# Attention into an MLP on one core: the MLP's elementwise work from GpSimd to VectorE, weights two steps ahead, the first block's x prepared over three head pairs

## The chip, the cores and the metric

The kernel runs on one core of a Trainium2 chip. The metric is the time of one execution on the device in microseconds, the median of the runs shown. One execution was also taken with the hardware profiler; every row below is from it. TensorE (PE) multiplies matrices, and its weight loads stand apart as PEld. VectorE is DVE, ScalarE is ACT, GpSimd is POOL, and SyncE (SP) issues nearly all DMA transfers, in the order in which they are written.

## The reference

Attention with a learned bias on relative positions, for 4 batches of 8 heads, 576 positions and 64 columns, and then an MLP over the 2304 tokens:

```python
scores = scale * np.matmul(q, k.transpose(0, 1, 3, 2))
scores = scores + bias.transpose(2, 0, 1)[None, :, :, :]
attn = np.exp(scores - np.max(scores, axis=-1, keepdims=True))
attn = attn / (np.sum(attn, axis=-1, keepdims=True) + 1e-09)
x = np.matmul(attn, v)            # heads side by side: 2304 x 512
h = x @ w_in                      # 512 x 2048
g = np.where(h > 0.0, h, np.exp(np.minimum(h, 0.0)) - 1.0)   # elu
out = g @ w_out                   # 2048 x 512
```

All tensors are float32. The kernel multiplies each in two parts, a high part (the value rounded to the matmul's format) and a low part (the value less its high part), in three products: high by high, high by low, low by high.

## The kernel before

The bias is built first. Attention then runs over 16 head pairs (0 to 15), each in five parts (`order`): scores on TensorE, the sum with the bias and its minimum on VectorE (line 303), the exponential on ScalarE (line 314), a copy of 64 columns on GpSimd (line 319), transposes and the product with v on TensorE. The finished rows go to DRAM (`xd`), as do the sums of the exponentials, inverted (`rd`). Beside that, `aside` decodes one of the 16 weight chunks per head pair and stores it (`wf`).

The MLP works on 3 blocks of 768 tokens (`j`). The 16 chunks of 128 features are taken two at a time, so there are 24 steps (`i`), eight to a block. Steps 0 and 1 (`eight`) compute four products of 12 matmuls. Steps 2 to 23 (`seven`) compute the same with seven products of 6 matmuls (Strassen's scheme), which wants sums of the weights (`make_w`, the tile S) and of x (`sums_x`: T1 to T4). A product goes to one of two PSUM banks (`bank`, h0 and h1); VectorE adds products (the tiles u and c, line 796), the elu is made of a product or sum (`elu_a`: ScalarE's exponential, two VectorE steps), and split into high (`gh`, ScalarE) and low (`gl`, VectorE) by `elu_b`. Between the products of a step stand the 36 matmuls of the second matrix of the step before (`second`, into six banks `acc`); after its last matmul a bank is copied to a tile `os` and stored.

`make_w` runs only in the first block, in step i-1 for step i: two chunks `wa` are loaded (line 490, 0.5 MB each), summed (lines 689 to 694), cast to high parts (ScalarE, line 686), and the low parts are taken (line 687; VectorE takes two, GpSimd three). The result, 2.8 MB, is kept for the step and stored to DRAM (lines 707 and 708); blocks 1 and 2 load it from there (`fetch_w`). The tiles `wa` have two buffers, so that the two chunks of the next step can be loaded only when GpSimd has taken the last low part of this one.

The x of a block is loaded in four pieces (`load_x`: xd into xr, rd into rr), scaled by rr (`scale_x`), split (`high_x`, `low_x`) and summed (`sums_x`). All of it is written out in an order fixed by hand: each engine gets its instructions in the order of the Python code, and waits in that order. `at(i, k, ...)` puts a call after product k of step i.

Of the kernel before, what the change touches and what calls it, by code (L numbers as in the profile page):

```python
# [24 lines left out]
def kernel(  # L25
# [484 lines left out]
    def attention():  # L510
# [16 lines left out]
        late = []  # L527

# [21 lines left out]
        for n in range(NP):  # L550
# [4 lines left out]
            for i, u in enumerate(order):  # L555
# [28 lines left out]
                at = (n - NP + 3, i)  # L584
# [8 lines left out]
                if at == (1, 4):  # L593
                    load_x(0, 1, 0)
                if not last:
                    continue
                if i == 0:
                    load_w(0)
                    load_w(1)
                    scale_x(0, 1, 0, nc.gpsimd)  # L600
                    high_x(0, "B11", xo["B11"], nc.vector.tensor_copy)
                if i == 1:
                    load_x(0, 1, 1)
                    low_x(0, "B11", xo["B11"], nc.gpsimd)
                if i == 2:
                    high_w(0)
                    high_x(0, "B21", xo["B21"], nc.vector.tensor_copy)
                    low_x(0, "B21", xo["B21"], nc.gpsimd)
                if i == 3:
                    low_w(0, nc.vector)  # L610
                    high_x(0, "B12", xo["B12"], nc.vector.tensor_copy)
                    low_x(0, "B12", xo["B12"], nc.gpsimd)
                if i == 4:
                    load_w(2)
                    scale_x(0, 1, 1, nc.gpsimd)
                    high_w(1)
                    decode(dp, plan.get(n), "scale")
        late += pv(NP - 1, 0, (0, 1, 2, 3, 4), xp)
        trans_mid(NP - 1, (2, 3))
        for _ in trans_p(NP - 1, order[-1]):  # L620
            pass
        high_x(0, "B22", xo["B22"], nc.vector.tensor_copy)
# [4 lines left out]

        for op in ("low", "sign", "shift", "add"):
            decode(dp, plan.get(NP - 1), op)
# [7 lines left out]
    def mlp():  # L637
# [7 lines left out]
        slots.extend(halves(xq.tile([P, 2 * XW], F32R, name=f"xs{i}")) for i in range(8 - len(slots)))  # L645
        AN, GN = 2 * 7 * AW, 4 * DM

        third = RW // 2
        wrings = [
            [wq.tile([P, n], F32R, name=f"{x}{i}") for i in range(2)] + [room[:, o:o + n]]  # L650
            for x, n, o in (("wA", AN, third), ("wB", GN, third + AN))
# [18 lines left out]
        def make_w(i):  # L670
# [7 lines left out]
            g = nc.gpsimd  # L678
# [8 lines left out]
            low = lambda k, eng: eng.tensor_sub(parts[k][1], parts[k][2], parts[k][0].bitcast(F32))  # L687
# [8 lines left out]
            low(0, nc.vector)  # L696
            yield
            high(4)
            low(1, nc.vector)
            yield  # L700
            high(2)
            high(3)
            low(4, g)
            yield
            low(2, g)
            low(3, g)
# [6 lines left out]
        def second(i, order):  # L713
            j = i // NQ
            for e, h in order:
# [4 lines left out]
                for t in range(3 * h, 3 * h + 3):  # L720
# [3 lines left out]
                    for x, w in ((gh, wh), (gh, wl), (gl, wh)):  # L724
# [8 lines left out]
                        if count[j, t] == 6 * NQ:  # L733
                            os = ep.tile([P, DM], F32, tag="os", name="os", bufs=2)
# [19 lines left out]

        def bank(k):
            return hp.tile([P, HB], F32, tag=f"h{k % 2}", name=f"h{k % 2}")
# [211 lines left out]
```

## Time and profile before

| | |
|---|---|
| median of 3 runs | 780.82 us (779.89 to 782.12) |
| the profiled execution | 779.03 us, its span 777.2 us |
| TensorE busy | 700.7 us, 90% of the span |
| VectorE busy | 495.7 us, 64% |
| ScalarE busy | 392.6 us, 51% |
| GpSimd busy | 209.9 us, 27% |
| TensorE's granted clock, mean | 0.957 of full |

The span is the time from the first to the last instruction; the execution's own time is 1.8 us longer. In rows of the trace a time in us stands first, then a duration in us, the engine, the line, the operation, what it writes and reads, and how many instructions were put together. In brackets is the engine's idle time just before, and who ended it.

### The profile page before, as it was taken

Reading aid. Unit: us, or ns where it says so; the run is one execution under the profiler, and the core shown is the slowest. Engines: PE = TensorE matmul, PEld = TensorE weight load, DVE = VectorE, ACT = ScalarE, POOL = GpSimd, SP = SyncE. Lnnn points to the kernel's source line nnn. Section 1 sums busy time; section 2 is a strip of 40 time slices with the busy share of each in tenths; the row PEclk is TensorE's granted clock in tenths of the full one; section 3 lists DMA queues with packets and bytes.
Section 4 is the critical chain, followed back from the end, with each engine's and each line's share of the span. In section 5 each row is a group of like instructions: output and inputs, shape, how many; then the busy total and the mean of one; then the engine's idle time right before and its main releaser. Section 6 shows DMA issues by size and latency. Waiting matters only on the chain.

```text
span 777.2 us, 13260 instructions
## 1 busy us (share of the span) xinstructions
PE 700.7 (90%) x4992; PEld 519.1 (67%) x4992; DVE 495.7 (64%) x955; ACT 392.6 (51%) x857; POOL 209.9 (27%) x193
## 2 busy tenths in 40 slices
PE   5998999999999989595888877759999999999996
PEld 3335555556556545495777766648889888989985
DVE  7986777767677764863666665754555676555553
ACT  6997778778877876342333334332222253233222
POOL 0002223222322237613555584530110420000000
PEclk9999999999999998888999987898999999999999
DMA  6997565545554676307666614756765544635302
GB/s 174 221 220 204 180 203 188 182 153 205 182 175 159 232 208 202 126 0 243 235 226 223 226 60 168 285 220 245 257 237 192 219 185 170 252 149 199 152 1 81
DMA packets 49935, 144.58 MB, mean 186 GB/s; under 512 B 13376, under 2 KB 26448, under 8 KB 42192
## 3 DMA queue, kind: packets, MB, share of 16 engines
q1 hardware_dynamic: 49136, 143.44, 55.0%
q8 instruction: 39, 0.64, 0.4%
q10 hardware_dynamic: 736, 0.31, 0.2%
q14 instruction: 24, 0.20, 0.1%
HBM read 92.14 MB, written 40.97 MB: 171 GB/s over the span
## 4 chain that ended last, share of the span: by engine, by line
PE 29%; DMA 10%; POOL 9%; DVE 4%; ACT 3%; issue 2%; SPq 2%; POOLq 0%; ACTq 0%; DVEq 0%
PE acc L726 15%; PE h L763 14%; DMA wa<-wf 8%; DMA out_dram<-os 2%; POOL wA L687 2%; DVE e L744 1%; SPq L490 1%; POOL bias L687 1%; POOL wB L687 1%; POOL S L693 1%; POOL S L694 1%; POOL S L690 1%; DVE e L745 1%; DVE gl L753 1%; POOL S L689 1%
## 5 line engine op out<-in xcount | busy, mean ns | idle before, releaser
L303 DVE CUSTOM_DVE_ANT_0 ss<-ps,bias 128x576 f32<-128x576 f32 x128 | 91.9, 755 | 74.3 <-PE ps L291 60.9
L763 PE MATMUL h<-bias,wA 128*128 128x384 f32 x480 | 104.1, 353 | 30.3 <-DVE c L796 16.8
L744 DVE TENSOR_SCALAR e<-e 128x384 f32<-128x384 f32 x96 | 54.7, 569 | 108.4 <-ACT e L743 108.4
L726 PE MATMUL acc<-wB,gh 128*128 128x512 f32 x360 | 120.6, 404 | 0.0
L763 PEld LDWEIGHTS h<-bias,wA 128*128 128x128 f32 x480 | 88.9, 196 | 43.9 <-issue 18.5
L314 ACT ACTIVATE ss<-ss,nm 128x576 f32<-128x576 f32 x128 | 98.2, 769 | 30.9 <-DVE nm L303 30.8
L291 PE MATMUL ps<-kk,qq 64*128 64x288 f32 (+1 forms) x640 | 108.8, 425 | 2.6 <-DVE nm L303 2.4
L752 ACT CAST gh<-e 128x384 fp32r<-128x384 f32 x96 | 49.3, 513 | 105.2 <-DVE e L745 101.7
L753 DVE TENSOR_TENSOR gl<-e,gh 128x384 fp32r<-128x384 f32 x96 | 68.5, 714 | 46.5 <-ACT gh L752 46.5
L763 PE MATMUL h<-bias 128*128 128x384 f32 x324 | 71.1, 363 | 18.9 <-DVE e L745 11.3
L743 ACT ACTIVATE e<-c 128x384 f32<-128x384 f32 x66 | 34.6, 524 | 102.7 <-DVE c L796 102.7
L763 PEld LDWEIGHTS h<-bias 128*128 128x128 f32 x324 | 62.5, 204 | 26.5 <-DVE e L745 12.6
L291 PEld LDWEIGHTS ps<-kk,qq 64*128 64x128 f32 (+1 forms) x640 | 63.4, 180 | 20.9 <-DVE nm L303 4.7
L726 PEld LDWEIGHTS acc<-wB,gh 128*128 128x128 f32 x360 | 69.5, 195 | 10.4
L319 POOL TENSOR_SCALAR ss<-ss 128x64 f32<-128x64 f32 x64 | 15.9, 249 | 221.0 <-ACT ss L314 221.0
L726 PE MATMUL acc<-wB,gl 128*128 128x512 f32 x180 | 72.4, 402 | 0.0
L726 PE MATMUL acc<-bias,gh 128*128 128x512 f32 x216 | 72.3, 404 | 0.0
L193 PE MATMUL bps<-rel,cs 128*32 128x288 f32 x576 | 44.9, 435 | 11.3 <-ACT rel L183 7.7
L399 PE MATMUL wv<-pta,vv 128*64 128x320 f32 (+1 forms) x320 | 53.6, 448 | 0.0
L355 PEld LDWEIGHTS wt<-ident,ss 64*128 64x128 f32 x1024 | 38.5, 141 | 18.9 <-issue 14.7
L796 DVE TENSOR_TENSOR c<-h,u 128x384 f32<-128x384 f32 x66 | 36.3, 550 | 18.3 <-PE h L763 18.1
L355 PE MATMUL wt<-ident,ss 64*128 64x64 f32 x1024 | 47.5, 231 | 0.0
(104 smaller groups left out, 1109.3 us busy)
## 6 DMA issues: line engine op xcount, KB each, us to landing
wA<-wA SPq DMA_DIRECT2D x15, 1792.0 KB
raw<-in_wd_dram SPq DMA_DIRECT2D x16, 1024.0 KB, 5.1
wB<-wB SPq DMA_DIRECT2D x15, 1024.0 KB, 4.8
wa<-wf SPq DMA_DIRECT2D x20, 512.0 KB, 8.5
bias<-bo SPq DMA_DIRECT2D x16, 576.0 KB, 7.4
bias<-wA SPq DMA_DIRECT2D x5, 1792.0 KB
wf<-da SPq DMA_DIRECT2D x16, 512.0 KB, 2.8
bias<-wB SPq DMA_DIRECT2D x5, 1024.0 KB, 4.6
```

The costliest lines, as they stand in the source:

```text
L193: nc.tensor.matmul(ps[32 * g:32 * g + 32, f, 0:HS], lhsT=W2, rhs=rel[g][:, f * HS:(f + 1) * HS], start=True, stop=True,)
L291: nc.tensor.matmul(banks[e][:, f, 0:HS] if u < NCH else banks[0][r, f, 0:HS], lhsT=qq[r, rows], rhs=kk[r, f * HS:(f + 1) * HS], start=True ...
L303: nc.vector.tensor_tensor_reduce(out=s.rearrange("p (f x) -> p f x", f=2), in0=ps[:, :, 0:HS], in1=bap.rearrange("p (f x) -> p f x", f=2), ...
L314: nc.scalar.activation(s, s, AF.Exp, bias=nm[:, e:e + 1], scale=-1.0, accum_out=sm[:, hp, col:col + 1])
L355: nc.tensor.transpose(banks[r][:, x * TAIL:(x + 1) * TAIL], ss[q, c:c + P], ident[q, q])
L399: nc.tensor.matmul(w[e * D:(e + 1) * D, 0:N], lhsT=l, rhs=r, start=(j == first), stop=(j == end))
L726: nc.tensor.matmul(acc[j, t], lhsT=x[:, t * P:(t + 1) * P], rhs=w, start=(count[j, t] == 1), stop=(count[j, t] == 6 * NQ),)
L744: nc.vector.tensor_scalar(e, e, 1.0, -1.0, op0=ALU.min, op1=ALU.add)
L752: nc.scalar.copy(gh, x)
L753: nc.vector.tensor_sub(gl, x, gh.bitcast(F32))
L763: nc.tensor.matmul(ps, lhsT=a[f][c], rhs=x[y][c], start=(start and k == 0), stop=(stop and k == len(todo) - 1), skip_group_check=not start,)
L796: nc.vector.tensor_add(u[name], x, y)
```

## The change

- `make_w`: the sums and all low parts are VectorE's; it is cut into seven pieces, so that the work is spread over the products of a step, and its stores to DRAM come at the next step's first product.
- `load_w` for step i is called after product 1 of step i-2 (before: product 6, for the first two steps product 3); every other step's chunks have tiles of their own (`wq`), so four chunks can be held.
- `elu_a`: with Relu of -h and the exponential of its negative on ScalarE, and one VectorE instruction (add -1, maximum with h).
- The second block's and third block's `scale_x`, `sums_x` and low parts are VectorE's; two of the seven x operands are split a step ahead (a ninth slot), the others a product earlier.
- The first block's x is loaded and scaled from head pair 12 on, by VectorE, and split on VectorE; its T1 to T4 are made on GpSimd in a row at the MLP's start.
- The last chunk's decoding stands before the last transposes; in step 0 the third and fourth product use PSUM banks of the pool `accp`; `os` has three buffers, not two.

```diff
-    def load_w(fc):
-        wa = wab[fc] = keep.tile([P, WW], F32, tag="wa", name="wa")
+    def load_w(fc, pool=None):
+        wa = wab[fc] = (pool or keep).tile([P, WW], F32, tag="wa", name="wa", bufs=2)
         nc.sync.dma_start(out=wa, in_=wf[fc])
...
+        early = {
+            (-4, 3): [(load_x, 0, 0, 0)],
+            (-3, 0): [(scale_x, 0, 0, 0, nc.vector)],
+            (-3, 1): [(load_x, 0, 0, 1)],
+            (-3, 4): [(scale_x, 0, 0, 1, nc.vector)],
+            (-2, 0): [(load_x, 0, 1, 0), (high_x, 0, "B11", xo["B11"], nc.vector.tensor_copy)],
+            (-2, 2): [(low_x, 0, "B11", xo["B11"], nc.vector)],
+            (-2, 3): [(scale_x, 0, 1, 0, nc.vector)],
+            (-2, 4): [(load_x, 0, 1, 1)],
+            (-1, 0): [(high_x, 0, "B12", xo["B12"], nc.vector.tensor_copy)],
+            (-1, 1): [(low_x, 0, "B12", xo["B12"], nc.vector), (scale_x, 0, 1, 1, nc.vector)],
+            (-1, 2): [(high_x, 0, "B21", xo["B21"], nc.vector.tensor_copy)],
+            (-1, 3): [(low_x, 0, "B21", xo["B21"], nc.vector)],
+        }
...
-                if at == (0, 3):
-                    load_x(0, 0, 0)
-                if at == (1, 0):
-                    scale_x(0, 0, 0, nc.gpsimd)
-                if at == (1, 2):
-                    load_x(0, 0, 1)
-                if at == (1, 3):
-                    scale_x(0, 0, 1, nc.gpsimd)
...
+                for fn, *args in early.get((n - NP, i), ()):
+                    fn(*args)
...
-            g.tensor_add(S1[:, 0], A21, A22)
-            g.tensor_sub(S1[:, 2], A11, A21)
+            v.tensor_add(S1[:, 0], A21, A22)
+            v.tensor_sub(S1[:, 2], A11, A21)
             high(0)
             yield
-            g.tensor_sub(S1[:, 1], S1[:, 0], A11)
-            g.tensor_sub(S1[:, 3], A12, S1[:, 1])
+            v.tensor_sub(S1[:, 1], S1[:, 0], A11)
+            v.tensor_sub(S1[:, 3], A12, S1[:, 1])
+            high(4)
+            yield
+            low(0)
             high(1)
...
-            nc.scalar.activation(e, src, AF.Exp)
-            nc.vector.tensor_scalar(e, e, 1.0, -1.0, op0=ALU.min, op1=ALU.add)
-            nc.vector.tensor_max(e, src, e)
+            nc.scalar.activation(e, src, AF.Relu, scale=-1.0)
+            nc.scalar.activation(e, e, AF.Exp, scale=-1.0)
+            nc.vector.scalar_tensor_tensor(e, e, -1.0, src, op0=ALU.add, op1=ALU.max)
...
-                at(i - 2, 3 if i - 2 < FIRST else 6, load_w, 2 * q + e)
-            for k in range(5):
-                at(i - 1, k if i > FIRST else min(k, 3), next, run)
-            at(i - 1, 5 if i > FIRST else 3, next, run, None)
+                at(i - 2, 1, load_w, 2 * q + e, wq if i % 2 == 0 else keep)
+            for k in range(7):
+                at(i - 1, k if i > FIRST else k // 2, next, run)
+            at(i, 0, next, run, None)
```

What this does to VectorE's order in a step of the first block, here in step 4, from the elu of the third product to the sum c of the sixth. In rows of this kind stand the line, the operation, what it writes and reads, and the size; line 796 of before is line 799 of the changed kernel, 687 is 685 there. Before:

```order
L744 TENSOR_SCALAR e<-e 128x384
L745 TENSOR_TENSOR e<-h_4980,e 128x384
L687 TENSOR_TENSOR wA_4420<-wa,wA_4420 128x512
L753 TENSOR_TENSOR gl<-e,gh 128x384
L796 TENSOR_TENSOR u_5052<-h_5006,p_4989 128x384
L687 TENSOR_TENSOR wB_4422<-wa,wB_4422 128x512
L796 TENSOR_TENSOR c<-h_5061,u_5052 128x384
L744 TENSOR_SCALAR e<-e 128x384
L745 TENSOR_TENSOR e<-c,e 128x384
L753 TENSOR_TENSOR gl<-e,gh 128x384
L796 TENSOR_TENSOR c<-h_5082,u_5052 128x384
```

And with the change, at the same place:

```order
L745 SCALAR_TENSOR_TENSOR e<-e,h_4978 128x384
L691 TENSOR_TENSOR S<-S,wa 128x256
L692 TENSOR_TENSOR S<-wa,S 128x256
L753 TENSOR_TENSOR gl<-e,gh 128x384
L799 TENSOR_TENSOR u_5055<-h_5006,p_4987 128x384
L685 TENSOR_TENSOR wA_4420<-wa,wA_4420 128x512
L799 TENSOR_TENSOR c<-h_5064,u_5055 128x384
L745 SCALAR_TENSOR_TENSOR e<-e,c 128x384
L685 TENSOR_TENSOR wA_4420<-S,wA_4420 128x1024
L753 TENSOR_TENSOR gl<-e,gh 128x384
L799 TENSOR_TENSOR c<-h_5085,u_5055 128x384
```

The clamp of line 744 is gone; two sums S and the low part of 128x1024 stand in VectorE's queue instead, the latter between an elu's maximum and its low part `gl`.

SyncE's transfers of a step of the first block (wA, wB: the stores; xr, rr: the next block's x; wa: chunks to come) stood so before:

```order
L707 DMA wA_4427<-wA_4421 128x3584
L708 DMA wB_4435<-wB_4423 128x2048
L490 DMA wa<-wf_90 128x1024
L490 DMA wa<-wf_91 128x1024
L448 DMA xr_4693<-xd_76 128x2x384
L452 DMA rr<-rd_80 64x2x384 x2
```

and stand so now:

```order
L707 DMA wA_4427<-bias 128x3584
L708 DMA wB_4435<-wB_4422 128x2048
L448 DMA xr_4693<-xd_76 128x2x384
L452 DMA rr<-rd_80 64x2x384 x2
L490 DMA wa<-wf_92 128x1024
L490 DMA wa<-wf_93 128x1024
```

The two chunks come behind the next block's x, and after the stores of the same step stand the loads for one step later than before (chunks 92 and 93 where 90 and 91 were; the names count from wf_82).

VectorE's queue in the last head pair, as a piece of the difference (line 303 is the scores' sum with the bias, 460 the scaling of x, 483 and 486 its high and low part):

```order
+L359 COPY pta<-wt 128x8x64
+L405 COPY xs<-wv 128x320
+L486 TENSOR_TENSOR bias<-xr_3599,bias 128x768
+L460 TENSOR_TENSOR xr_3921<-xr_3921,rr 128x2x384
 L303 ISA st_112,nm<-ps,biast 128x576
 L303 ISA nm 128x1
-L483 CAST bias<-xr_4084 128x768
```

A low part and a scaling now stand ahead of the third part's line 303 (the two copies above them only look new: they stood there before).

## Rows read from the trace of the kernel before

**Rows 1.** Busy us by stretch: length, PE, PEld, DVE, ACT, POOL; clock, DMA share, GB/s.
```profile
390.00:410.00 20.00, 17.18 (x78) 14.61 (x77) 12.65 (x19) 7.29 (x14) 10.27 (x8) 0.91 0.68 235
...
450.00:470.00 20.00, 15.44 (x60) 12.11 (x59) 14.97 (x17) 6.21 (x12) 17.67 (x11) 0.83 0.25 105
...
570.00:590.00 20.00, 20.00 (x101) 18.00 (x100) 11.29 (x23) 5.91 (x12) 1.84 (x1) 1.00 0.70 238
```

**Rows 2.** TensorE in time: first products of steps 2, 4, 10, 11 and 18.
```profile
350.76 1.23 PE L763 MATMUL h<-bias,wA 128*128 128x384 f32 x6
...
398.68 1.68 PE L763 MATMUL h<-bias 128*128 128x384 f32 x6 [2.82 <-DVE c L796]
...
538.19 1.21 PE L763 MATMUL h<-bias 128*128 128x384 f32 x6
...
553.95 1.21 PE L763 MATMUL h<-bias,wA 128*128 128x384 f32 x6
...
667.66 1.21 PE L763 MATMUL h<-bias,wA 128*128 128x384 f32 x6
```

**Rows 3.** Chain of waits, step 4 and the start of the next turn.
```profile
399.36 8.74 DMA wa<-wf
...
416.64 1.55 POOL wB L687
...
419.90 8.63 DMA wa<-wf
```

**Rows 4.** GpSimd in time, steps 3 and 4: idle before it in brackets.
```profile
392.90 2.40 POOL L687 TENSOR_TENSOR bias<-S,bias 128x1024 fp32r<-128x1024 f32 x1 [1.16 <-ACT bias L686]
...
408.24 0.74 POOL L689 TENSOR_TENSOR S<-wa 128x256 f32<-128x256 f32 x1 [8.49 <-DMA wa<-wf]
```

**Rows 5.** VectorE in time, step 3, beside GpSimd's 392.90 row.
```profile
393.28 2.24 DVE L744 TENSOR_SCALAR e<-e 128x384 f32<-128x384 f32 x1 [1.67 <-ACT e L743]
```

**Rows 6.** VectorE in time, step 12: one elu, from sum to sum.
```profile
579.82 0.56 DVE L796 TENSOR_TENSOR c<-h,u 128x384 f32<-128x384 f32 x1 [1.30 <-PE h L763]
...
581.03 0.36 DVE L744 TENSOR_SCALAR e<-e 128x384 f32<-128x384 f32 x1 [0.65 <-ACT e L743]
...
581.42 0.56 DVE L745 TENSOR_TENSOR e<-c,e 128x384 f32<-128x384 f32 x1
...
582.56 0.56 DVE L753 TENSOR_TENSOR gl<-e,gh 128x384 fp32r<-128x384 f32 x1 [0.58 <-ACT gh L752]
...
583.04 0.55 DVE L796 TENSOR_TENSOR c<-h,u 128x384 f32<-128x384 f32 x1
```

**Rows 7.** VectorE and ScalarE in time: prices of single operations.
```profile
304.80 1.22 DVE L497 TENSOR_TENSOR bias<-wa,bias 128x1024 fp32r<-128x1024 f32 x1
...
341.96 0.95 DVE L486 TENSOR_TENSOR xs<-xr,xs 128x768 fp32r<-128x768 f32 x1
...
391.78 1.05 ACT L686 CAST bias<-S 128x1024 fp32r<-128x1024 f32 x1 [2.96 <-POOL S L694]
...
580.47 0.52 ACT L743 ACTIVATE e<-c 128x384 f32<-128x384 f32 x1 [3.01 <-DVE c L796]
```

**Rows 8.** Last head pair: a stretch, GpSimd in time, TensorE in time.
```profile
285.00:300.00 15.00, 10.26 (x92) 5.98 (x90) 5.59 (x14) 7.35 (x18) 7.25 (x7) 0.77 0.76 214
...
290.83 1.80 POOL L460 TENSOR_TENSOR xr<-xr,rr 128x768 f32<-128x768 f32 x1 [6.55 <-DMA rr<-rd]
...
292.90 0.48 PE L340 MATMUL wm<-ident,ss 128*128 128x128 f32 x1 [4.74 <-POOL ss L319]
```

**Rows 9.** TensorE in time: the products of step 0 and the first of step 1.
```profile
315.18 4.43 PE L763 MATMUL h<-bias 128*128 128x384 f32 x24 [0.47 <-DVE rs L332]
...
322.84 3.04 PE L763 MATMUL h<-bias 128*128 128x384 f32 x12 [3.22 <-DVE e L745]
...
329.56 6.71 PE L763 MATMUL h<-bias 128*128 128x384 f32 x24 [3.69 <-DVE e L745]
```

**Rows 10.** VectorE in time: a copy of the output, at the end.
```profile
770.04 0.69 DVE L735 COPY os<-acc 128x512 f32<-128x512 f32 x1 [2.20 <-DMA out_dram<-os]
```

More of the change, by code (lines that the diff above doesn't have):

```diff
@@ L599, in attention @@
                     load_w(1)
[L600 to L604, printed above, removed]
                 if i == 2:
                     high_w(0)
-                    high_x(0, "B21", xo["B21"], nc.vector.tensor_copy)
-                    low_x(0, "B21", xo["B21"], nc.gpsimd)
                 if i == 3:
                     low_w(0, nc.vector)
-                    high_x(0, "B12", xo["B12"], nc.vector.tensor_copy)
-                    low_x(0, "B12", xo["B12"], nc.gpsimd)
                 if i == 4:
                     load_w(2)
-                    scale_x(0, 1, 1, nc.gpsimd)
                     high_w(1)
                     decode(dp, plan.get(n), "scale")
+        decode(dp, plan.get(NP - 1), "low")
+        decode(dp, plan.get(NP - 1), "sign")
+        decode(dp, plan.get(NP - 1), "shift")
         late += pv(NP - 1, 0, (0, 1, 2, 3, 4), xp)
@@ L621, in attention @@
             pass
+        decode(dp, plan.get(NP - 1), "add")
         high_x(0, "B22", xo["B22"], nc.vector.tensor_copy)
@@ L626, in attention @@
         low_w(1, nc.vector)
-        for op in ("low", "sign", "shift", "add"):
-            decode(dp, plan.get(NP - 1), op)
         for fn in late:
@@ L645, in mlp @@
         slots.extend(halves(xq.tile([P, 2 * XW], F32R, name=f"xs{i}")) for i in range(8 - len(slots)))
+        slots.append(halves(room[:, RW - 2 * XW:]))
         AN, GN = 2 * 7 * AW, 4 * DM
-        third = RW // 2
         wrings = [
-            [wq.tile([P, n], F32R, name=f"{x}{i}") for i in range(2)] + [room[:, o:o + n]]
-            for x, n, o in (("wA", AN, third), ("wB", GN, third + AN))
+            [wq.tile([P, AN], F32R, name="wA0")] + [room[:, o:o + AN] for o in (RW // 2, RW // 2 + 4 * WW)],
+            [wq.tile([P, GN], F32R, name=f"wB{i}") for i in range(3)],
         ]
@@ L686, in make_w @@
             high = lambda k: nc.scalar.copy(parts[k][0], parts[k][2])
-            low = lambda k, eng: eng.tensor_sub(parts[k][1], parts[k][2], parts[k][0].bitcast(F32))
+            low = lambda k: v.tensor_sub(parts[k][1], parts[k][2], parts[k][0].bitcast(F32))
             yield
-            g.tensor_add(S1[:, 0], A21, A22)
-            g.tensor_sub(S1[:, 2], A11, A21)
+            v.tensor_add(S1[:, 0], A21, A22)
+            v.tensor_sub(S1[:, 2], A11, A21)
             high(0)
             yield
-            g.tensor_sub(S1[:, 1], S1[:, 0], A11)
-            g.tensor_sub(S1[:, 3], A12, S1[:, 1])
+            v.tensor_sub(S1[:, 1], S1[:, 0], A11)
[3 more added lines that the diff above has]
+            low(0)
             high(1)
-            low(0, nc.vector)
             yield
-            high(4)
-            low(1, nc.vector)
-            yield
+            low(4)
             high(2)
             high(3)
-            low(4, g)
             yield
-            low(2, g)
-            low(3, g)
+            low(1)
+            low(2)
+            yield
+            low(3)
+            yield
             nc.sync.dma_start(out=wA[q], in_=ta.bitcast(F32))
@@ L755, in bank @@
         def bank(k):
+            if k > 3:
+                return accp.tile([P, DM], F32, tag="acc", name="acc")[:, 0:HB]
             return hp.tile([P, HB], F32, tag=f"h{k % 2}", name=f"h{k % 2}")
@@ L776, in eight @@
                 b1, b2 = (xo[f"B{r}{h + 1}"] for r in (1, 2))
-                ps = bank(k)
+                ps = bank(k + 2 if i == 0 and k > 1 else k)
                 product(
@@ L836, in mlp @@
         xo.update(zip(("T1", "T2", "T3", "T4"), slots[4:]))
-        free = [slots[1]]
-        for k, name in enumerate(("T1", "T3", "T2", "T4")):
-            at(0, k, sums_x, 0, (name,), G)
-            at(1, k, high_x, 0, name, xo[name], nc.scalar.copy)
-            at(1, k, low_x, 0, name, xo[name], V)
-        at(0, 0, high_w, 3)
-        at(0, 0, low_w, 3, V)
+        free = [slots[8], slots[1]]
+        for name in ("T1", "T3", "T2", "T4"):
+            sums_x(0, (name,), G)
+        at(0, 0, high_w, 3)
+        at(0, 1, low_w, 3, V)
+        for k, name in enumerate(("T1", "T3", "T2", "T4")):
+            m = (0, 3) if k == 0 else (1, k - 1)
+            at(*m, high_x, 0, name, xo[name], nc.scalar.copy)
+            at(*m, low_x, 0, name, xo[name], V)
         made = range(FIRST, NQ + FIRST)
@@ L881, in aside @@
                     if k in (2, 3, 4, 5):
[L882 removed]
+                        sums_x(j + 1, (("T1", "T3", "T2", "T4")[k - 2],), V)
+                    if k == 6:
+                        turn_x(j + 1, 1)
                 if j + 1 < NB and q == NQ - 1:
                     free.append(xo[PRODS[k][1]])
[L885 to L886 removed]
+                    if k < 5:
+                        turn_x(j + 1, k + 2)
             late, order = eight(i, rest, aside) if i < FIRST else seven(i, rest, aside, late)
```

14 lines of the change are left out of this document (4 added, 10 removed).

## The prediction

> **What bounds the kernel now.** I read three views in this order: busy time by stretch, TensorE in time, and the chain of waits. In block 1 (570 to 590 us) TensorE is busy all the time at full clock, so no elementwise edit can speed that up; in block 0 (390 to 410, 450 to 470) it is busy 17.2 and 15.4 us of 20, at 0.91 and 0.83 of the clock [rows 1]. The reader should see steps there: a clean one takes 553.95 - 538.19 = 15.8 us, but steps 2 to 9 took 538.19 - 350.76 = 187.4 us where eight clean ones take 126 [rows 2]. That gap of 61 us is the prize. Block 1 lost little: 667.66 - 538.19 = 129.5 us for eight steps.
>
> The chain of waits shows why. Chunks land 8.7 us after the chain enters their transfer, GpSimd and ScalarE work on them, GpSimd's last low part ends at 418.2 and only then does the next transfer start: from 399.36 to 419.90, 20.5 us a turn [rows 3]. GpSimd itself idles 8.5 us of it, waiting for chunks [rows 4]. Inside such a step TensorE stands 2.8 us for a sum c of VectorE's [rows 2], and VectorE is late because of GpSimd: its clamp of 128x384 took 2.24 us while GpSimd's low part ran for 2.40, against 0.36 alone [rows 4 to 6]. Two more places lose time. In the last head pair GpSimd waits 6.55 us for rr, the small copy (line 319) queued behind it comes late, and TensorE stands 4.74 us and then runs at 0.77 of the clock [rows 8]. In step 0 it stands 3.22 and 3.69 us for elus, since there are two banks [rows 9].
>
> **The change part by part.** Prices first. VectorE's operations overlap a little: 582.56 + 0.56 ends 0.08 after the next began [rows 6]. So its queue pays 0.48 for 128x384, 0.87 for 128x768 and 1.14 for 128x1024 [rows 6, 7]; by the same line 0.61 for 512 columns and 0.35 for 256.
>
> *Block 0, steps 2 to 9.* With four chunks held, the next load no longer waits for the last low part of the same turn: it has a whole step for its 8.7 us and the wait for it goes. What is late next is VectorE, whose queue now alternates with ScalarE. One elu loop, sum to sum, is 583.04 - 579.82 = 3.22 us [rows 6]. The change takes out the clamp (581.42 - 581.03 = 0.39) and puts in a second ScalarE pass, 0.52 plus a hand-over of 0.04 [rows 6, 7], so 3.39. The fused instruction I price as the maximum that it replaces (0.56). Between it and gl lies a gap of 0.66 (0.58 waiting, 0.08 overlap), where low parts hide. From the fifth product on:
>
> - sum 5 to 6: the low part of 1024 is 1.14, so 0.48 over the gap: 3.87;
> - sum 6 to 7: low parts of 512 and 256, 0.96, so 0.30 over: 3.69;
> - sum 7 to the next step: 0.61, hidden: 3.39;
> - u and two S sums: 0.48 + 0.70 = 1.18;
> - the third product's maximum 0.48 and two S sums 0.70; then gl waits for ScalarE, which first casts the sums (1.05 [rows 7]) and then gh (about 0.55), with hand-overs 0.1; gl, u and a low part of 512, 0.48 + 0.48 + 0.61: together 4.45.
>
> Sum 16.6 us, over the 15.8 of TensorE, so VectorE paces. Steps 3 to 6 also scale x (0.87): 17.4. Step 6 has four x sums and two low parts more, 6 x 0.87, one of which fits where gl waits for ScalarE: 21.7. Step 7 has five low parts, again one hidden: 20.1. Step 8 is 16.6, step 9 makes no weights: 15.8. Steps 2 to 9: 16.6 + 3 x 17.4 + 21.7 + 20.1 + 16.6 + 15.8 = 143.0, and I take 145, for waits on ScalarE's other casts. That is -42. Bounds: TensorE alone, 126 (-61); and no better than today's turn of 20.5 in every step, 164, plus the 10 us of x work in steps 6 and 7, 174 (-13). I stay near the sum, since each term has a row.
>
> *The start, steps 0 and 1.* From 315.18 to 350.76 they take 35.6 us. With four banks step 0 is two runs of 24 products at 4.43, 8.9 us; step 1, from about 333 (half of the last run of 24) to 350.76, is 17.8 and stays [rows 9, 2]. So 26.7: -9. What could fill that hole: the T sums on GpSimd beside VectorE's first low parts and elus. Bounds: -10, and 0 if those stretch as the clamp did.
>
> Here the Trainium skill says something sharper (SBUF — State Buffer, Who interferes with whom): of a VectorE operation with two SBUF inputs and a GpSimd operation that reads SBUF, the one that comes second waits until the other is done. The rows 4 and 5 agree: 2.24 us, ended just after GpSimd's operation did. By it VectorE would get about one operation in for each of the sums, and the start would win some 3 us less; in block 0, where GpSimd has nothing left, it would take nothing.
>
> *The last head pairs.* TensorE's idle 4.74 goes, and the slow clock after it: 10.26 busy us at 0.77, some 2.4. But VectorE now waits for rr itself, with the scores' sums (line 303) queued behind, in head pair 13 and in the last: I keep 2 us of the 7.1 as lost. -5, bounds 0 and -7.
>
> *Blocks 1 and 2 and the end.* GpSimd's sums leave VectorE alone at block 1's end, where 129.5 - 126 = 3.5 us are lost: -2 (0 to -3.5). The elu saves VectorE time that TensorE hides there: nothing; without that cover it would be the 0.17 longer loop. The third `os` buffer takes one of the final waits of 2.20 [rows 10]: -2 (0 to -2.2).
>
> Sum: -42 - 9 - 5 - 2 - 2 = -60. The profiled execution took 779.03, its span 777.2; it becomes 719. The median of the runs lay 1.8 above it, so I predict **721 us**.
>
> **The rivals.**
>
> *TensorE paces after all.* If VectorE's queue catches up in the first products of each step, where TensorE gives slack, steps fall to near 15.8 except 6 and 7: 126 + 8 = 134, 11 us less: 710. For it: VectorE's waits in my sum are hand-overs that today's 3.22 loops carry without loss in block 1. Against: my sum leaves no idle stretch to catch up in.
>
> *The loads stay late.* They now follow the next block's x on SyncE and share the transfer engines with 2.8 MB of stores. DMA's share in block 0 is 0.68 at 20.5 us a step [rows 1]; at 17.4 it is 0.80. If chunks land too late for the S sums, VectorE's whole queue stands, elus with it, and steps return to about 20.5: 6 steps x 3.5 = 21 more, 742.
>
> *The first x and the start win nothing,* because VectorE waits for rr as GpSimd did and the T sums stretch the first elus: 12 us more, 733.
>
> *Slower than before.* Gaps in each step cost TensorE its clock: after standing 2.82 us, six products took 1.68 against 1.21 [rows 2]. If a gap in every VectorE-paced step held it at the lower of its levels (1.2 of 2.4 GHz), steps would near 31.5 us, eight of them 252, and the time would be about 828. It decides from 187.4 + 18 = 205 us for the eight steps, 25.7 each, that is, at the lower level for some two thirds. Against: a slower TensorE closes its own gaps, and the stretch with turns of 20.5 us still had 0.91. The Trainium skill describes such a kernel (TensorE: Matmul & The Clock Gate, A second HAM failure mode: psum-queue depth-cycling), short idles between groups of matmuls that make the clock go back and forth; the rows show it only after gaps of 2.8 us and more.
>
> **How the numbers follow.** My forecast, VectorE pacing block 0 at 16.5 to 18 us a step: 0.53, 712 to 731. TensorE pacing: 0.14. Late loads: 0.14. Nothing won ahead of block 0: 0.12. Slower by the clock: 0.04, and within 0.3%, which is about what runs of this kernel can tell from no change, 0.03, for mixtures of late loads and a lost clock. Faster 0.93. Range 704 to 744, which takes in the first three rivals.
>
> **What would show it.** Right: steps 2 to 9 of some 145 us with GpSimd empty in them; VectorE's clamp row gone and no VectorE row of 128x384 above 0.6 us after step 0; the chain of waits in block 0 passing through VectorE and ScalarE, not through the transfers of wa; no idle of TensorE for line 319 in the last head pair; step 0 in about 9 us. Wrong: VectorE waiting for wa or rr by microseconds in block 0, TensorE's clock under 0.9 there, or steps 6 and 7 above 25 us.

## The result, and the profile after

The changed kernel takes **726.66 us** (median of 4 runs, 724.77 to 729.18), the kernel before 780.91 in the same series: ratio 0.9307, 95% interval 0.9275 to 0.9338. Forecast were 721 us and a range of 704 to 744. The profiled execution took 726.57 us, its span 724.8, 52.4 less than before. TensorE is now busy for 94% of it, GpSimd for 11% (before 27%).

Stretches of the trace after, those of [rows 1, 8] and the one behind the last; the columns are the stretch, its length, busy time of TensorE, weight loads, VectorE, ScalarE and GpSimd, the granted clock, DMA's share and GB/s:

```profile
285.00:300.00 15.00, 15.00 (x154) 8.93 (x154) 13.00 (x28) 11.15 (x30) 4.58 (x5) 1.00 0.73 226
300.00:315.00 15.00, 10.91 (x105) 5.88 (x104) 13.70 (x19) 10.15 (x23) 8.27 (x6) 1.00 0.31 108
390.00:410.00 20.00, 18.83 (x92) 16.30 (x91) 13.56 (x26) 11.32 (x23) 0.00 (x0) 1.00 0.85 267
450.00:470.00 20.00, 17.07 (x83) 14.49 (x82) 13.39 (x25) 11.73 (x24) 0.00 (x0) 1.00 0.60 236
```

In block 0 (390 to 410) the clock is whole, GpSimd is empty and DMA's share is up from 0.68 to 0.85. The stretch before 300, where TensorE stood and then ran at 0.77, is full. The hole has moved to 300 to 315, where TensorE is busy for 10.91 us (before: 14.13).

TensorE in time after the change: the first products of steps 0, 2, 10 and 18 (316.56, 343.28, 490.32, 617.29), and products that had to wait.

```profile
316.56 5.99 PE L766 MATMUL h<-bias 128*128 128x384 f32 x24 [2.17 <-DVE rs L332]
322.39 4.32 PE L766 MATMUL acc<-bias 128*128 128x384 f32 x24
...
343.28 1.23 PE L766 MATMUL h<-bias,wA 128*128 128x384 f32 x6
...
362.95 1.31 PE L766 MATMUL h<-bias 128*128 128x384 f32 x6 [1.01 <-DVE c L799]
...
476.25 1.31 PE L766 MATMUL h<-bias 128*128 128x384 f32 x6 [1.63 <-DVE c L799]
...
490.32 1.21 PE L766 MATMUL h<-bias 128*128 128x384 f32 x6
...
617.29 1.21 PE L766 MATMUL h<-bias 128*128 128x384 f32 x6
```

Differences of these starts and of those in [rows 2, 9] split the 52.4 us as the prediction split its sum:

| stretch | before | after | measured | forecast |
|---|---|---|---|---|
| up to the MLP's first product | 315.18 | 316.56 | +1.4 | -5 |
| steps 0 and 1 | 35.6 | 26.7 | -8.9 | -9 |
| steps 2 to 9 | 187.4 | 147.0 | -40.4 | -42 |
| steps 10 to 17 | 129.5 | 127.0 | -2.5 | -2 |
| step 18 to the end | 109.5 | 107.5 | -2.0 | -2 |

Four of the five lines came within 2 us. The first one came 6.4 us off, which is most of the 7.6 by which the measured 52.4 falls short of the forecast 60. (For the median the forecast had added 1.8 us to the profiled execution's 719; after the change the two agree within 0.1, so it was 5.7 off.) All these starts are of one execution of each kernel.

### The profile page after: what moved, and what is told of

Its sections match the earlier page's. It is cut to its first block, busy times and chain, and to the rows that moved or that the text cites. A ratio compares the mean times of both kernels' runs of the same rounds, so it can differ in the third digit from the quotient of the medians.

```text
span 724.8 us, 13195 instructions
## 1 busy us (share of the span) xinstructions
PE 684.8 (94%) x4992; PEld 507.1 (70%) x4992; DVE 475.0 (66%) x946; ACT 441.9 (61%) x953; POOL 81.7 (11%) x106
## 4 chain that ended last, share of the span: by engine, by line
PE 61%; DVE 16%; ACT 14%; DMA 4%; issue 3%; SPq 1%; POOL 0%; DVEq 0%; ACTq 0%; POOLq 0%
PE acc L726 16%; PE h L766 15%; PE ps L291 11%; PE wv L399 11%; PE wt L355 5%; ACT bo L206 3%; DVE e L745 3%; ACT e L743 2%; ACT e L744 2%; DVE gl L753 2%; DVE c L799 2%; ACT rel L183 2%; PE wm L340 1%; DVE bias L486 1%; DVE bias L685 1%
## 5 line engine op out<-in xcount | busy, mean ns | idle before, releaser
L726 PE MATMUL acc<-wB,gh 128*128 128x512 f32 x528 | 172.1, 394 | 0.0
L766 PE MATMUL h<-bias 128*128 128x384 f32 x552 | 114.8, 346 | 11.7 <-DVE c L799 8.7
L766 PEld LDWEIGHTS h<-bias 128*128 128x128 f32 x552 | 100.6, 192 | 23.6 <-DVE c L799 8.7
L726 PE MATMUL acc<-wB,gl 128*128 128x512 f32 x264 | 104.4, 395 | 0.0
L745 DVE SCALAR_TENSOR_TENSOR e<-e,c 128x384 f32<-128x384 f32 x66 | 36.9, 559 | 75.8 <-ACT e L744 75.8
L766 PE MATMUL h<-bias,wA 128*128 128x384 f32 x276 | 56.8, 341 | 4.3 <-DVE c L799 3.8
L766 PEld LDWEIGHTS h<-bias,wA 128*128 128x128 f32 x276 | 49.5, 188 | 10.2 <-DVE c L799 2.9
L726 PEld LDWEIGHTS acc<-wB,gl 128*128 128x128 f32 x264 | 49.8, 188 | 7.8
L744 ACT ACTIVATE e<-e 128x384 f32<-128x384 f32 x96 | 50.5, 526 | 3.0
L355 PEld LDWEIGHTS wt<-ident,ss 64*128 64x128 f32 x1024 | 37.8, 139 | 19.6 <-issue 14.6
L399 PE MATMUL wv<-ptb,vv 128*64 128x256 f32 (+1 forms) x320 | 46.3, 394 | 2.0 <-DVE xs L405 2.0
```

Of the source, the lines that this page charges most:

```text
L355: nc.tensor.transpose(banks[r][:, x * TAIL:(x + 1) * TAIL], ss[q, c:c + P], ident[q, q])
L399: nc.tensor.matmul(w[e * D:(e + 1) * D, 0:N], lhsT=l, rhs=r, start=(j == first), stop=(j == end))
L726: nc.tensor.matmul(acc[j, t], lhsT=x[:, t * P:(t + 1) * P], rhs=w, start=(count[j, t] == 1), stop=(count[j, t] == 6 * NQ),)
L744: nc.scalar.activation(e, e, AF.Exp, scale=-1.0)
L745: nc.vector.scalar_tensor_tensor(e, e, -1.0, src, op0=ALU.add, op1=ALU.max)
L766: nc.tensor.matmul(ps, lhsT=a[f][c], rhs=x[y][c], start=(start and k == 0), stop=(stop and k == len(todo) - 1), skip_group_check=not start,)
```

## The experiments

Three series of four kernels, three rounds each beside the kernel before (its medians: 781.69, 779.66, 780.2). None leaves out any computation. Line numbers shift by a few between them. Times in us are compared as medians; since the kernel before itself differs by 2 us between the series, a difference of 1 to 2 us between kernels of different series tells nothing. The measure "end" is the time from GpSimd's last scaling of the scores (the copy of line 319, written as a scaling by 1) to the MLP's first product; it is free of what happens earlier in attention, where the last scaling itself came at 303.4 to 309.0 in kernels with the same x code.

| kernel | end | steps 0, 1 | each of 3 to 5 | steps 2 to 9 | median us | ratio, interval |
|---|---|---|---|---|---|---|
| after the change | 10.5 | 26.7 | 17.5 | 147.0 | 726.66 | 0.9307, 0.9275 to 0.9338 |
| e1 old elu | 10.5 | 27.3 | 17.1 | 146.6 | 725.74 | 0.9309, 0.9266 to 0.9353 |
| e2 T sums by VectorE | 7.3 | 25.8 | 17.4 | 147.6 | 723.70 | 0.9269, 0.9234 to 0.9304 |
| e3 weights by GpSimd | 10.4 | 27.3 | 18.9 | 155.6 | 732.84 | 0.9385, 0.9352 to 0.9419 |
| e4 loads one step ahead | 10.3 | 26.7 | 19.8 | 165.7 | 744.33 | 0.9533, 0.9499 to 0.9567 |
| e5 first x as before | 12.4 | 26.7 | 17.5 | 146.8 | 731.70 | 0.9389, 0.9372 to 0.9406 |
| e6 gh first | 10.5 | 27.3 | 16.4 | 139.5 | 717.62 | 0.9202, 0.9188 to 0.9216 |
| e8 T by VectorE, B22 by ScalarE | 6.8 | 25.1 | 17.5 | 147.4 | 721.00 | 0.9248, 0.9234 to 0.9262 |
| e9 e6 and e8 | 6.8 | 25.4 | 16.4 | 139.8 | 713.77 | 0.9156, 0.9142 to 0.9170 |
| e10 decoding as before | 6.3 | 29.0 | 17.5 | 148.1 | 724.91 | 0.9294, 0.9263 to 0.9324 |
| e11 e9 and e10 | 6.3 | 29.7 | 16.4 | 138.6 | 716.56 | 0.9182, 0.9148 to 0.9216 |
| e12 e9, old elu | 6.8 | 26.5 | 16.1 | 139.0 | 714.61 | 0.9146, 0.9103 to 0.9189 |
| e13 two banks in step 0 | 10.4 | 30.6 | 17.4 | 146.5 | 730.14 | 0.9348, 0.9320 to 0.9377 |

**Theory A**: in block 0 VectorE and ScalarE, taking turns, now pace the step, and the late transfer was the larger part of the old turn; at the end of attention GpSimd's additions, which the change moved there, hold up VectorE. Each run has a rival of its own.

### Block 0: which part won it

**e1**, the elu alone undone:

```diff
-            nc.scalar.activation(e, src, AF.Relu, scale=-1.0)
-            nc.scalar.activation(e, e, AF.Exp, scale=-1.0)
-            nc.vector.scalar_tensor_tensor(e, e, -1.0, src, op0=ALU.add, op1=ALU.max)
+            nc.scalar.activation(e, src, AF.Exp)
+            nc.vector.tensor_scalar(e, e, 1.0, -1.0, op0=ALU.min, op1=ALU.add)
+            nc.vector.tensor_max(e, src, e)
```

> Only the elu goes back to one ScalarE pass and two VectorE steps. Theory A (in block 0 VectorE and ScalarE take turns, and the length of the loop counts, not VectorE's busy time): the old elu's loop is about 0.1 us shorter, four elus a step, so a step of 17.47 us becomes about 17.1, and the time falls by 2 to 4 us. Rival (VectorE's busy time counts, and the clamp, 0.28 us of its queue, comes back four times a step): steps of about 18.5, the time 7 us longer.

Steps 3 to 5 took 17.0 to 17.2 against 17.5, so theory A holds on the step and the rival falls; but the whole time differs by 0.9 us, less than either kernel's runs differ among themselves. The new elu won nothing here: the clamp it removes was slow only beside GpSimd [rows 5, 6], which is empty now.

**e3**, the sums and three low parts of the weights on GpSimd again, the loads still two steps ahead:

```diff
-            v.tensor_add(S1[:, 0], A21, A22)
-            v.tensor_sub(S1[:, 2], A11, A21)
+            g.tensor_add(S1[:, 0], A21, A22)
+            g.tensor_sub(S1[:, 2], A11, A21)
...
-            low(4)
+            low(4, g)
```

> The four sums and three of the low parts of make_w go back to GpSimd; the loads stay two steps ahead. Theory A (the transfer in the loop was the larger part of the 20.5 us turn): steps 3 to 5 take 18 to 19 us, VectorE stretched beside GpSimd, the time 5 to 12 us longer than with the change. Rival (GpSimd was the loop): steps of 20.5 us again, the time 22 us longer or more.

18.9 a step and +6.2 us, as A has it. VectorE of e3 in time, where GpSimd's low part started at 386.75 and took 2.40:

```profile
387.12 2.45 DVE L753 TENSOR_TENSOR gl<-e,gh 128x384 fp32r<-128x384 f32 x1 [0.80 <-ACT gh L752]
```

The same instruction takes 0.56 alone: what GpSimd takes off VectorE's queue it gives back, and more, by holding up what VectorE does meanwhile.

**e4**, VectorE makes the weights, but the loads stand at their old places:

```diff
-                at(i - 2, 1, load_w, 2 * q + e, wq if i % 2 == 0 else keep)
+                at(i - 2, 3 if i - 2 < FIRST else 6, load_w, 2 * q + e)
```

> The chunks are loaded at the old places, one step ahead, in two buffers; VectorE makes sums and low parts as in the change. Theory A (the transfer stood in the loop, and VectorE's queue is spread over a whole step): a load waits for the last low part, VectorE for the load, so a turn is some 15 us of VectorE's work plus 7 to 9 of loading: steps of 22 to 25 us, worse than the 20.5 before any change, the time about 35 to 50 us longer than with the change. Rival (GpSimd's slowness was the cost): steps of 18 us or less, the time within 5 us of the change's.

The rival (within 5 us) falls, +17.7. A's size was missed too: steps of 19.8, not 22 to 25. VectorE of e4 in time, the first sum of a step's weights:

```profile
390.36 0.42 DVE L687 TENSOR_TENSOR S<-wa 128x256 f32<-128x256 f32 x1 [2.45 <-DMA wa<-wf]
```

It waits 2.45 us for its chunk, no more: chunks land in 4.9 us here (median), and took 8.5 in the kernel before. The DMA part of the page, for the kernel after (KB each, median us from issue to landing):

```profile
wa<-wf SPq DMA_DIRECT2D x20, 512.0 KB, 4.6
```

**e6**, on ScalarE the operand that the elu writes (gh) ahead of the sums' high part:

```diff
-            high(4)
             yield
+            high(4)
             low(0)
             high(1)
```

> ScalarE casts the operand elu writes (gh) before it casts the sums' high part, where the kernel after does it the other way. Theory A (block 0's steps are a chain between VectorE and ScalarE, in which VectorE waits 1.53 for gh each step): the wait goes, steps 3 to 5 fall from 17.47 to 15.9 to 16.4, block 0's eight steps from 147 to 136 to 140, and the time is 717 to 720. Rival (VectorE's own work or TensorE paces the step, and the wait only moves to another place): steps 3 to 5 stay at 17.1 to 17.5 and the time within 2 us of 726.7.

VectorE of the kernel after in time, step 4, where S has been summed and gl has to wait for gh:

```profile
386.42 0.42 DVE L692 TENSOR_TENSOR S<-wa,S 128x256 f32<-128x256 f32 x1
388.37 0.56 DVE L753 TENSOR_TENSOR gl<-e,gh 128x384 fp32r<-128x384 f32 x1 [1.53 <-ACT gh L752]
...
389.91 0.55 DVE L799 TENSOR_TENSOR c<-h,u 128x384 f32<-128x384 f32 x1
...
393.69 0.55 DVE L799 TENSOR_TENSOR c<-h,u 128x384 f32<-128x384 f32 x1
```

ScalarE of the same kernel there: it takes up the cast of the sums (1.05) first, then gh.

```profile
386.88 1.05 ACT L684 CAST wA<-S 128x1024 fp32r<-128x1024 f32 x1 [1.42 <-DVE S L692]
387.83 0.51 ACT L752 CAST gh<-e 128x384 fp32r<-128x384 f32 x1
```

And the same place in e6, VectorE:

```profile
383.35 0.43 DVE L692 TENSOR_TENSOR S<-wa,S 128x256 f32<-128x256 f32 x1
383.70 0.55 DVE L753 TENSOR_TENSOR gl<-e,gh 128x384 fp32r<-128x384 f32 x1
```

No wait is left, steps 3 to 5 take 16.4, block 0 139.5 and the kernel 717.62 us. The step falls by 1.1, not by the full 1.5. The rival falls: the order of two casts on ScalarE was worth some 8 us. Steps 2 to 9 fell by 7.6, and 0.9202 against 0.9307 of the kernel before is 8.2; the medians differ by 9.0, but they are of two series.

### The end of attention and the start of the MLP

Here `sm` is the sums of the exponentials, which VectorE inverts; TensorE transposes them, and VectorE copies the result to `rs`. B22 is the last of the four pieces of the first block's x. VectorE of the kernel after in time, the last instructions of attention:

```profile
308.32 0.69 DVE L265 TENSOR_SCALAR da<-da 128x1024 uint32<-128x1024 uint32 x1 [1.23 <-POOL da L255]
308.93 0.48 DVE L405 COPY xs<-wv 128x320 f32<-128x320 f32 x1
309.33 2.54 DVE L483 CAST bias<-xr 128x768 fp32r<-128x768 f32 x1
311.79 1.78 DVE L324 TENSOR_SCALAR sm<-sm 128x36 f32<-128x36 f32 x1
...
313.89 2.33 DVE L486 TENSOR_TENSOR bias<-xr,bias 128x768 fp32r<-128x768 f32 x1
```

GpSimd of the same kernel there: the last scaling, the decoding's addition (line 268), the first two T sums (line 474).

```profile
306.09 1.11 POOL L319 TENSOR_SCALAR ss<-ss 128x64 f32<-128x64 f32 x1 [2.45 <-ACT ss L314]
...
309.10 2.35 POOL L268 TENSOR_TENSOR da<-da,dm 128x1024 int32<-128x1024 int32 x1 [0.81 <-DVE da L265]
311.40 2.12 POOL L474 TENSOR_TENSOR xr<-xr 128x768 f32<-128x768 f32 x1
313.61 1.80 POOL L474 TENSOR_TENSOR xr<-xr,xr 128x768 f32<-128x768 f32 x1
```

Three times an instruction of VectorE lies beside one of GpSimd and ends only when that has ended. The scaling of 36 columns takes 1.78; with nothing beside it in e10 it takes 0.18. Behind it TensorE waits 2.04 for `sm` and 2.17 for `rs`, and its next 24 matmuls take 5.99 in place of 4.32, at a granted clock of 0.71 (316.56 to 322.39).

**e2**, the T sums of the first block by VectorE, one after each product of step 0:

```diff
-        for name in ("T1", "T3", "T2", "T4"):
-            sums_x(0, (name,), G)
         at(0, 0, high_w, 3)
         at(0, 1, low_w, 3, V)
+        for k, name in enumerate(("T1", "T3", "T2", "T4")):
+            at(0, k, sums_x, 0, (name,), V)
```

> Only the first block's four T sums change: VectorE makes them, one after each product of step 0, so that GpSimd has nothing after the last chunk's decoding. Theory A (the T sums on GpSimd held up the VectorE work for which the first products wait): the low part of B22 and the copy of rs take 0.9 and 0.3 us right after each other, the first product of the MLP starts 3 to 4 us earlier than 316.56, step 0 is no longer than 10.5 us, and the time falls by about 3 us. Rival (VectorE's own longer queue at the end of attention was the delay): the start stays within 1 us, the time the same or longer by the 3.5 us of the four sums.

The time is as A expected, 3.0 less. The first product came only 1.4 earlier, since in this execution the last scaling came 1.8 later than in the kernel after; from there the end took 7.3 in place of 10.5, the 3.2 that A named.

**e8**, e2 and B22's cast on ScalarE:

```diff
-        high_x(0, "B22", xo["B22"], nc.vector.tensor_copy)
+        high_x(0, "B22", xo["B22"], nc.scalar.copy)
```

> As the run with the first block's T sums on VectorE, and B22's high part is cast by ScalarE too, so that no VectorE cast of x runs beside GpSimd's addition of the mask. Theory A (the end of the last pair waits for VectorE instructions that are held up beside GpSimd: the cast took 2.54 there, 0.56 alone): from the last scaling of the scores to the MLP's first product 5.0 to 6.0 us, where the run with T on VectorE alone had 7.30 and the kernel after 10.47; time 721 to 723. Rival (the hold-up moves to the instruction that is next beside GpSimd's addition): 7 us again, time 723 to 725.

The end is 6.8, not A's 5.0 to 6.0: here the rival was right, though the time is A's (the intervals of e2 and e8 overlap). The hold-up moves on. VectorE of e9, which has the same end, beside GpSimd's addition (307.97, 2.37):

```profile
308.21 2.17 DVE L324 TENSOR_SCALAR sm<-sm 128x36 f32<-128x36 f32 x1
```

ScalarE of e9 at the same time, with the cast that took VectorE 2.54:

```profile
308.61 0.84 ACT L483 CAST bias<-xr 128x768 fp32r<-128x768 f32 x1
```

The Trainium skill (SBUF — State Buffer, Who interferes with whom) names two kinds of VectorE instruction that GpSimd shuts out, and that shut it out, for a whole instruction: those with two SBUF inputs, beside a GpSimd instruction that reads SBUF, and single-input copies, casts and scalings in a mode that uses both of VectorE's ports; ScalarE waits for neither. The runs agree, down to a VectorE instruction of 36 columns. The cast, the scaling and the clamp of [rows 5] read one operand, so they belong under the second kind, not under the first, with which the prediction compared the clamp.

**e10**, the change, but the decoding of the last chunk behind the last low part, where it stood before:

```diff
-        decode(dp, plan.get(NP - 1), "low")
-        decode(dp, plan.get(NP - 1), "sign")
-        decode(dp, plan.get(NP - 1), "shift")
...
-        decode(dp, plan.get(NP - 1), "add")
...
         low_w(1, nc.vector)
+        for op in ("low", "sign", "shift", "add"):
+            decode(dp, plan.get(NP - 1), op)
```

> The decoding of the last weight chunk (VectorE's three steps and GpSimd's addition) goes back behind the last low part of attention, as before the change; all else, the early x and the T sums on GpSimd too, is as after it. Theory A (the decoding that the change moved ahead holds VectorE 1.23 for GpSimd, in front of the copy that TensorE needs, and puts GpSimd's addition and T sums beside VectorE's last instructions): from the last scaling of the scores to the MLP's first product 6 to 7 us, as before the change, where the kernel after has 10.47; the T sums run beside step 0 again; time 722 to 725. Rival (what is won there is lost in steps 0 and 1, whose elus run beside the T sums again): the first product comes earlier as said, but steps 0 and 1 take 29 to 31 us in place of 26.7, and the time is within 1.5 us of 726.7.

The end takes 6.3 us, the length it had before the change, so the 4.2 us that the change lost there come from the place of the decoding and of the T sums queued behind its addition. Of these, 2.3 are lost again in steps 0 and 1 (29.0), where the T sums now hold up the elus: VectorE of e10 in time, beside GpSimd's T4 (324.26, 2.71):

```profile
325.19 2.20 DVE L751 TENSOR_TENSOR gl<-e,gh 128x384 fp32r<-128x384 f32 x1
```

So both named part of it; the net is -1.8 us, less than the runs can tell (0.9294 against 0.9307, intervals that overlap).

**e5**, the first block's x as in the kernel before (the table `early` with the old positions and GpSimd as the engine):

```diff
-            (-4, 3): [(load_x, 0, 0, 0)],
-            (-3, 0): [(scale_x, 0, 0, 0, nc.vector)],
...
-            (-1, 1): [(low_x, 0, "B12", xo["B12"], nc.vector), (scale_x, 0, 1, 1, nc.vector)],
...
+            (-3, 3): [(load_x, 0, 0, 0)],
+            (-2, 0): [(scale_x, 0, 0, 0, nc.gpsimd)],
...
+            (-1, 4): [(scale_x, 0, 1, 1, nc.gpsimd)],
```

> The first block's x is loaded and scaled as in the kernel before, on GpSimd in the last two head pairs; all else is as in the kernel after the change. Theory A (the early x does shorten the last head pairs, its gain being eaten by GpSimd's operand sums beside VectorE): the first mean matmul of the last pair started 3.6 us earlier after the change, so without the early x the first product of the MLP comes 2 to 5 us later than in the kernel after (316.6 there), 318 to 321, and the time is 728 to 731. Rival (the early x wins nothing; the head pairs are paced by the load of rr and by TensorE): the first product stays at 314 to 317 and the time within 1.5 us of 726.7.

The first product came at 322.25, 5.7 later than with the early x, and the time is 5.0 longer: the early x pays, a little over A's range; the rival falls. Of the 5.7, 1.9 lie behind the last scaling (12.4 against 10.5), the other 3.8 ahead of it, where single executions scatter. TensorE of e5 in time:

```profile
315.24 4.15 PE L399 MATMUL wv<-ptb,vv 64*64 64x256 f32 x20 [2.94 <-DVE xs L405]
...
322.25 5.97 PE L764 MATMUL h<-bias 128*128 128x384 f32 x24 [2.18 <-DVE rs L332]
```

**e13**, two PSUM banks for step 0, as before:

```diff
-                ps = bank(k + 2 if i == 0 and k > 1 else k)
+                ps = bank(k)
```

> The kernel after the change, with two PSUM banks for the four products of step 0, as before it. Theory A (step 0 was long before because its elus ran beside GpSimd's T sums; with those moved ahead an elu is done by the time its bank is needed): step 0 stays at 10 to 11 us, time within 2 us of 726.7. Rival (the banks gave the start its 9 us): step 0 takes 13 to 17 us and the time is 730 to 734.

Theory A falls, the rival holds at its low end: step 0 takes 13.2 us, steps 0 and 1 together 30.6, 3.9 more. TensorE of e13 in time, the fourth product:

```profile
327.63 6.21 PE L766 MATMUL h<-bias 128*128 128x384 f32 x24 [1.85 <-DVE e L745]
```

The elu it waits for stood behind a `gl` that VectorE took 1.60 for, beside a T sum of GpSimd's (324.88, 1.82), and that in turn behind a cast of ScalarE's that waited for a weight chunk:

```profile
323.59 1.05 ACT L493 CAST bias<-wa 128x1024 fp32r<-128x1024 f32 x1 [1.32 <-DMA wa<-wf]
```

With four banks that wait is covered.

### Put together

**e9** has the edits of e6 and e8.

> T sums on VectorE, B22's high part on ScalarE and gh cast first, in one kernel. Theory A: the gains of the three add up, as they lie in different stages: 726.7 less 3 less 2 less 8, 712 to 717. Rival (with gh first the steps of block 0 are bound by VectorE, which has the T sums only in step 0, so only the two gains at the end of attention remain): 720 to 723.

713.77 us (713.17 to 714.61): 12.9 less than the kernel after, where e6 alone is 9.0 less and e8 5.7. The gains nearly add up, as A expected; the rival falls. e9 beats both kernels, the one before by 8.4%, the changed one by 1.6% (0.9156 over 0.9307).

**e11** is e9 with e10's edit.

> The kernel with T on VectorE, B22's high part on ScalarE and gh first, and with the decoding at its old place as well. Theory A (what is left of the hold-up is GpSimd's addition beside the scaling of the sums, 2.17 us, and VectorE's wait of 1.24): from the last scaling of the scores to the first product 5.5 to 6.2 us where it has 6.84, time 712 to 714. Rival (VectorE now has the decoding and the T sums in step 0 one behind the other): steps 0 and 1 get 2 us longer and the time is 715 to 717.

The end is 6.3, half a us shorter, but steps 0 and 1 take 4.2 us longer: the decoding, the T sums and the elus now stand in one queue. The rival holds, 716.56, though by the time alone e9 and e11 can't be told apart (their intervals overlap).

**e12** is e9 with e1's edit.

> The kernel with T on VectorE, B22's high part on ScalarE and gh first, and the old elu (one pass on ScalarE, two instructions on VectorE). Theory A (block 0's steps are a chain of elu loops, and the old loop is some 0.1 us shorter): steps 3 to 5 fall by 0.2 to 0.4 from 16.39, time 711 to 713. Rival (with the wait for gh gone VectorE's number of instructions sets the step, and the old elu has seven more of 0.4 us in each): steps 3 to 5 of 17 to 19, time 718 to 730.

Steps 3 to 5 take 16.1 us each, 0.3 less, as A expected; the rival falls. The time, 714.61 (710.02 to 717.04), is over the 711 to 713 of theory A and can't be told from e9's: in the profiled execution the last scaling came at 308.98, 3.9 later than in e9.

## Why the prediction was right, and where it was off

**The mechanism held.** Four of the five signs named for "right" are there: steps 2 to 9 of 147 us with GpSimd empty; no VectorE row of 128x384 above 0.6 after step 0; no idle of TensorE for line 319 in the last pair; and the chain of waits goes through VectorE and ScalarE, not through `wa`. The fifth, step 0 in about 9 us, came to 10.0. The chain of the kernel after, in step 4, shows the turns (start, length, what):

```profile
389.91 0.56 DVE c L799
390.48 0.02 issue
390.50 0.54 ACT e L743
391.03 0.02 issue
391.06 0.53 ACT e L744
391.59 0.02 issue
391.61 0.56 DVE e L745
392.17 1.14 DVE wA L685
393.31 0.47 DVE gl L753
```

**Block 0's terms.** The loop with the low part of 1024 was put at 3.87 and took 393.69 - 389.91 = 3.78. Steps 2 to 9 were put at 16.6, three of 17.4, 21.7, 20.1, 16.6, 15.8, and took 16.3, three of 17.5, 19.6, 22.6, 18.0, 18.2. Steps 6 and 7 share their x work otherwise than I had it, with the same sum. The last two are 3.8 us longer: I left out the copies of finished output (`os`, line 735), which stand in the queues of VectorE and ScalarE in these steps, 0.68 just ahead of the gl and c for which TensorE waited 1.63 at 476.25. I also took step 9 for one that makes no weights, but the last three low parts stand in VectorE's queue after its first product (0.68, 0.42 and 0.69, from 473.64 on). The 2 us that I had added for other casts covered half of it.

**Where the 40.4 us lay.** The sum for block 0 is right as a length; as a reading of where the time went it is not. Step by step, before and after: step 2 took 27.4 and 16.3, steps 3 to 5 20.5 and 17.5 each, step 6 22.6 and 19.6, step 7 31.2 and 22.6, step 8 19.9 and 18.0, step 9 24.7 and 18.2. The turn of 20.5 that the prediction explains is that of steps 3 to 5, which gave 9 us; steps 2, 7 and 9 gave 26.4. In step 2 of the kernel before, TensorE waited 7.45 for an elu whose exponential stood on ScalarE behind a cast that waited 13.09 for a weight chunk. In step 9 it waited 5.48 for a copy on ScalarE that stood behind a copy to `os`, which waited 6.04 for a store. ScalarE and TensorE of the kernel before in time:

```profile
365.80 0.62 ACT L686 CAST wA<-wa 128x512 fp32r<-128x512 f32 x1 [13.09 <-DMA wa<-wf]
367.85 2.29 PE L763 MATMUL h<-bias,wA 128*128 128x384 f32 x6 [7.45 <-DVE e L745]
...
523.46 0.58 ACT L735 COPY os<-acc 128x512 f32<-128x512 f32 x1 [6.04 <-DMA out_dram<-os]
524.89 2.29 PE L763 MATMUL h<-bias,wA 128*128 128x384 f32 x6 [5.48 <-ACT p L811]
```

After the change TensorE waits 0.23 at most in step 2 and 1.63 in step 9, and nothing there waits for a store. The third `os` buffer, which the prediction prices only at the end of the kernel, may thus be worth more here; no run took it back. Step 7 had the second block's x work on GpSimd, and no run put that back either.

**The failed step** is "The last head pairs. TensorE's idle 4.74 goes, and the slow clock after it ... -5, bounds 0 and -7". It measured +1.4, outside its bounds. What it speaks of did happen: TensorE is full and at full clock from 285 to 300, VectorE waits 3.13 for rr in head pair 13, and the last scaling of scores came at 306.09, 2.9 earlier than before (308.97); undoing the early x cost 5.0. What it left out is the rest of the change in the same place: the decoding and the T sums, now ahead of the first product, make the way from that scaling to it 10.5 in place of 6.2, 4.3 more, and 4.3 - 2.9 = 1.4. The 4.3 is firm: the end takes 10.3 to 10.5 in all five runs with the same code there. The 2.9 is one execution against one, and kernels with the same early x reached the last scaling 2.7 earlier to 2.9 later than this one. e10 shows the cause by giving back 4.2, e2 that the T sums alone are 3.2 of it. I had named them as a danger to step 0 ("the T sums on GpSimd beside VectorE's first low parts and elus") and costed the moved decoding, which I had listed in the change, at nothing.

**The start** came to -8.9 for the -9, and that is luck in part: step 0 took 10.0 in place of 8.9, slow at first after TensorE's idles (clock 0.71), step 1 16.7 in place of 17.8. The prediction gave the whole -9 to the four banks, which are worth 3.9 (e13); where the T sums stand is worth another 2.3 (e10), and the rest was not separated.

**The rivals.** Late loads fell, but they are what e4 brings back, 17.7 us of the forecast 21. TensorE does not pace: it waits 1.01 for c in every step from 3 to 5 (362.95 above is step 3's). The clock held in spite of those gaps, at 1.00 from 350 to 430 and 0.91 from 430 to 450. "The first x and the start win nothing" was half right: the start won, the first x's gain was eaten.

**What each part is worth alone**, by undoing it: the loads 17.7, GpSimd's weights 6.2, the early x 5.0, the banks 3.5, the elu nothing; the moved decoding costs 1.8 at most. That is some 31 of the 54 us. For the rest there are two explanations: parts that stand in for each other (with the loads early, GpSimd's sums hurt less), and parts that no run undid, the second and third block's x work and the third `os` buffer above all. No run undid two parts together or either of these, so this stays open.

## What to carry to other kernels

Cost each instruction that a change moves at its new place, also those that the change's description doesn't name: the largest error here was an int addition and two sums on GpSimd that came to lie beside the last few VectorE instructions on the path. When two engines hand one operand back and forth, put the instruction that the other one waits for ahead of bulk work in each queue; here this one swap won some 8 us, about as much as the early x and the banks together (5.0 and 3.5). An edit that takes out an instruction which was slow only by its neighbour can be worth nothing once the neighbour is gone (e1). A sum can come out right while the time lay elsewhere: look at every step of the kernel before, not only at the one that repeats.

## What was not expected of the hardware

- A VectorE instruction of 128x36 elements took 1.78 and 2.17 us beside GpSimd's additions, 0.18 alone. The hold-up was as long as that of instructions more than ten times its size (2.20 and 2.45 for 128x384).
- The 0.5 MB loads landed in 4.6 us at a DMA share of 0.85, in 8.5 before at 0.68: a busier queue was not a slower one. The order on SyncE is what differs in the traces: in the kernel before, two chunks were issued at 398.09, right behind 2.8 MB of stores (issued at 396.13 and 397.67); after the change two were issued at 404.26, further behind such stores (396.95 and 400.20); in e4 they stand ahead of the stores and landed in 4.9. No run changed that order alone, so the cause stays open.
- The same attention code reached its last scaling between 303.4 and 309.0 us in different executions. VectorE's wait for rr in head pair 13 ran from 2.1 to 4.0 us, but not in step with it (e13: a wait of 2.17 and 307.35; e9: 3.30 and 305.10); the cause is open, and single starts in that stretch are good to a few us only.
